# An attention and mixer kernel on one core: the planner's durations and hand-over times reset, and a new table of places

## The chip, the core and the metric

One core of a Trainium2 chip runs the whole program. Its engines work side by side, each through its own list of instructions in order: TensorE (PE in the profile: matrix products, and transposes as products with an identity), VectorE (DVE), ScalarE (ACT), GpSimd (POOL) and SyncE (SP, which issues most DMAs). An instruction waits until the semaphores of what it depends on are up; whatever is queued behind it on its engine waits too. The metric is device time in microseconds (us) of one execution.

## The reference

The input is a sequence of 2048 rows of 512 numbers. Two layers with the same weights follow one another, each of two parts:

- A: `x + attention(layernorm(x)) @ wo`. Queries, keys and values are `layernorm(x) @ wqkv`, 32 heads of 16. Row s attends to the 8 rows s, s-2, ..., s-14 (rows below 0 masked), by softmax.
- B: with y the sum that A returns, `x = y + B(layernorm(y))`. In B, `h = gelu(layernorm(y') @ w1)` of its input y'; the four quarters of h's columns are shifted by +1, -1, +2 and -2 rows and multiplied by w2; `x1 = y' + that`; the result is `x1 + gelu(layernorm(x1) @ w3) @ w4`, with 1792 hidden columns.

All in float32.

## The kernel before

The 2048 rows are four blocks of 512, each four tiles of 128 rows; with two layers that makes eight block passes, n = 0 to 7. A pass goes through these stages, which the names in the code follow:

- `p1_stream` (for n = 0: `p1_quarters`): normalise, turn the tiles by TensorE transposes (`turn_pe`, four 128x128 transposes, shown as `mm<-ident,f`), multiply by wqkv (`mm<-wq_hl,xt`), scale into `ev`, write to DRAM.
- `p2_unit`: attention on VectorE for a quarter of the heads at a time: a product of 128x2048 (`prod<-kv,q`), a reduction (`L<-prod`), softmax, a second product and additions; the result o is turned (`mm<-ident,o`) into oT.
- `p3`: wo product (`mm<-wo_hl,oT`), sum with x on VectorE, norm, transposes (into `nT`), w1 product (`mm<-nT,w_hl`), gelu, shifts on GpSimd.
- `p4`: w2 product (`mm<-w_hl,h`), sum, norm, transposes.
- `p5`: 14 chunks of w3 product (`mm<-nT,w`), gelu, and w4 product into four accumulators (`acc<-w,g`).

Numbers are split into a high and a low float16 part, and a product is three float16 products (`HLS`), so one 128x512 result takes 12 matmuls; such a dozen is called a group below. Where `p3` and `p4` normalise a tile, the chain is: a group on TensorE; the sum on VectorE (`scalar_tensor_tensor`, which also sums the row); the square on ScalarE (`sq_dev`, L646); three tiny GpSimd instructions for the inverse root and the shift (`power`, L652; in the profile `b` in `p3` and `c` in `p4`); the normalised rows on ScalarE (`normed`, L665, writing `f`, or `prod` where a buffer is lent); four transposes on TensorE; eviction into `nT` on ScalarE. Whatever TensorE has queued between the group and the transposes covers that chain.

At the start the weights are scaled by a power of two and split (`small_weight`, `big_pair`), beside the first block's attention.

What sets the order: the code builds about 3150 operations (`Graph.__call__`, L210). Operation number k gets as its key the k-th number of the table `PLACES`. `plan` (L253) then plays the program forward: five engines, each with a time at which it is free; an operation is ready when its predecessors have ended and a hand-over time has passed; a free engine starts the ready operation of the lowest key whose buffers are to be had. Each operation's duration is the number given where it is made. `LAT` is the hand-over time, `LAT_PE` that to TensorE and `LAT_SP` that to SyncE from another engine. GpSimd operations, and VectorE operations marked "lock", exclude one another in the plan (`port`). Some operations may run on either of two engines, and the plan's choice is kept. The instructions are emitted in the order in which the plan starts them, and class `InOrder` (L360) holds each engine to it. The plan's times reach the chip only as this order. All instructions carry one line in the profile, that of `issue` (L370 before, L372 in the changed kernel), so they are told apart by their tiles.

Of the kernel before, what the change touches and what calls it, by code (L numbers as in the profile page):

```python
# [12 lines left out]
AF = mybir.ActivationFunctionType  # L13
ALU = mybir.AluOpType
# [6 lines left out]
D = 512  # L21
F = 1792
NB = 4
NT = 4
NC = D // P
# [180 lines left out]
class Graph:  # L206
# [3 lines left out]
    def __call__(self, key, alts, r=(), w=(), after=(), xfer=0.0):  # L210
# [30 lines left out]
        for b in o.touch:  # L241
            b.users += 1
            b.left += 1
        self.ops.append(o)
        return o


LAT, LAT_PE, LAT_SP, LAT_DMA, TABLE = 0.12, 0.4, 0.3, 2.3, 1.3
FREE = (7.0, 1.0, 1.5, 1.0, 1.1)
LANES = 8  # L250


def plan(ops, slots):  # L253

# [1121 lines left out]
```

## Time and profile before

| | |
|---|---|
| three runs | 1204.16, 1207.10, 1209.59 us; median 1207.1 |
| profiled execution, span | 1203.0 us, 15906 instructions |
| busy PE / DVE / ACT / POOL | 1178.4 / 926.1 / 639.6 / 355.9 us |
| stages of the span | 0 to 34 start; 34 to 132 weights and first attention; 132 to 205 first `p3`, `p4`; 205 to 431 passes 0 to 1 and the start of 2; 431 to 1198 the rest; 1198 to 1203 last store |

A row of the timeline gives start, duration, engine, operation, output tile, input tiles, and in brackets how long the engine stood idle before it and what ended that. Neighbouring like instructions are merged (x24 is two groups). Ends of matmuls are modelled and a little late: the spacing of starts is what TensorE took.

### The profile page before, as it was taken

The numbers are of one execution on the slowest core, as the hardware profiler recorded it, in microseconds if no ns is written. First come the engines' busy times: TensorE is split into PE (matmuls) and PEld (weight loads), VectorE is DVE, ScalarE is ACT, GpSimd is POOL, SyncE is SP. The second block draws the span as 40 slices with busy tenths as digits, with TensorE's granted clock in tenths as the row PEclk, the third lists the DMA queues.
The fourth block names the chain that finished last, engine by engine and source line by source line (L and its number), as shares of the span: only waits on it lengthen the run. The fifth ranks groups of instructions, "written<-read, shape, count | busy, mean of one in ns | idle before, by whom it ended". The sixth has DMA issues, their size and how long they took to land.

```text
span 1203.0 us, 15906 instructions
## 1 busy us (share of the span) xinstructions
PE 1178.4 (98%) x5652; PEld 586.9 (49%) x5652; DVE 926.1 (77%) x1082; ACT 639.6 (53%) x1118; POOL 355.9 (30%) x512
## 2 busy tenths in 40 slices
PE   8998999999999999999999999999999999999998
PEld 6544444554444445444444444444444444445554
DVE  4899898999899989888883799889897989324212
ACT  5755675236864374565564556544654554544331
POOL 4231344005611355143531163113612350221000
PEclk9999999999999999999999999999999999999999
DMA  7677775576695554554355446656248534111322
GB/s 204 200 214 203 217 201 143 158 201 166 187 273 171 156 148 100 157 138 118 100 149 134 138 130 179 173 140 171 60 140 188 150 101 149 62 53 66 102 79 62
DMA packets 129839, 176.77 MB, mean 147 GB/s; under 512 B 11704, under 2 KB 73144, under 8 KB 129760
## 3 DMA queue, kind: packets, MB, share of 16 engines
q1 hardware_dynamic: 127504, 173.86, 51.8%
q10 hardware_dynamic: 2256, 1.90, 0.6%
q8 instruction: 44, 0.72, 0.2%
q14 instruction: 35, 0.29, 0.1%
HBM read 132.64 MB, written 37.87 MB: 142 GB/s over the span
## 4 chain that ended last, share of the span: by engine, by line
PE 90%; DMA 3%; ACT 3%; POOL 1%; DVE 1%; issue 1%; SPq 1%; ACTq 0%; POOLq 0%; DVEq 0%
PE mm L370 67%; PE acc L370 24%; DMA w<-in_A_x_dram 1%; ACT junk L370 1%; SPq L370 1%; DMA h<-in_A_wqkv_dram 1%; DMA x<-in_A_x_dram 0%; DMA nT<-in_A_wqkv_dram 0%; ACT ev L370 0%; ACT f L370 0%; POOL c L370 0%; POOL x L370 0%; DMA w<-in_B_w_dram 0%; POOL b L370 0%; ACT xt L370 0%
## 5 line engine op out<-in xcount | busy, mean ns | idle before, releaser
L370 PE MATMUL acc<-w,g 128*128 128x512 f16 (+1 forms) x1260 | 307.6, 393 | 0.1
L370 PE MATMUL mm<-nT,w 128*128 128x512 f16 (+1 forms) x1288 | 304.6, 390 | 0.9 <-ACT nT L370 0.9
L370 PE MATMUL mm<-wq_hl,xt 128*128 128x512 f16 x1008 | 226.7, 381 | 3.8 <-ACT ev L370 3.8
L370 ACT ACTIVATE mm<-mm,s_w 128x512 f32<-128x512 f32 (+1 forms) x144 | 90.6, 630 | 207.3 <-PE mm L370 206.6
L370 PEld LDWEIGHTS <-w 128*128 128x128 f16 x1344 | 125.0, 98 | 136.6
L370 PEld LDWEIGHTS <-g 128*128 128x128 f16 x1176 | 115.0, 98 | 129.3
L370 PEld LDWEIGHTS <-xt 128*128 128x128 f16 x1008 | 99.2, 99 | 118.6 <-issue 7.3
L370 DVE TENSOR_TENSOR prod<-kv,L 128x2048 f32<-128x2048 f32 x64 | 147.2, 2299 | 0.8
L370 DVE TENSOR_REDUCE L<-prod 128x128 f32<-128x2048 f32 x64 | 145.9, 2281 | 0.5
L370 DVE TENSOR_TENSOR prod<-kv,q 128x2048 f32<-128x2048 f32 x58 | 134.0, 2310 | 3.3 <-DMA kv<-kv_d 2.3
L370 DVE TENSOR_TENSOR prod<-prod 128x1024 f32<-128x1024 f32 (+1 forms) x129 | 134.4, 1042 | 2.7
L370 POOL TENSOR_TENSOR g<-f,g 128x512 f16<-128x512 f32 x32 | 46.4, 1452 | 172.6 <-ACT f L370 103.2
L370 PE MATMUL mm<-nT,w_hl 128*128 128x512 f16 x384 | 87.9, 379 | 1.8 <-ACT nT L370 1.4
L370 PE MATMUL mm<-w_hl,h 128*128 128x512 f16 x384 | 86.0, 379 | 0.0
L370 PE MATMUL mm<-wo_hl,oT 128*128 128x512 f16 x384 | 85.3, 379 | 0.0
L370 DVE SCALAR_TENSOR_TENSOR g<-mm,c_g,g 128x512 f16<-128x512 f32 x56 | 41.8, 747 | 55.8 <-ACT g L370 55.7
L370 POOL TENSOR_SCALAR b<-b 128x1 f32<-128x1 f32 (+1 forms) x48 | 20.4, 425 | 191.2 <-ACT junk L370 189.4
L370 DVE TENSOR_TENSOR nT<-mm,nT 128x512 f16<-128x512 f32 x60 | 40.8, 687 | 45.1 <-ACT nT L370 44.5
L370 ACT ACT_TABLE_LOAD x54 | 69.3, 1283 | 6.6 <-issue 3.6
L370 ACT ACTIVATE ev<-mm,s_kv 128x512 f32<-128x512 f32 x56 | 38.3, 684 | 62.1 <-PE mm L370 49.4
L370 ACT ACTIVATE g<-mm,c_g 128x512 f16<-128x512 f32 x98 | 66.9, 685 | 2.0
L370 POOL COPY h<-h 128x126 f16<-128x126 f16 (+3 forms) x56 | 42.8, 786 | 81.7 <-DVE h L370 79.7
(189 smaller groups left out, 1408.0 us busy)
## 6 DMA issues: line engine op xcount, KB each, us to landing
w<-w SPq DMA_DIRECT2D x196, 256.0 KB
kv<-kv_d SPq DMA_DIRECT2D x112, 352.0 KB
w<-in_B_w_dram SPq DMA_DIRECT2D x56, 256.0 KB
kv_d<-ev SPq DMA_DIRECT2D x112, 128.0 KB
q_d<-ev SPq DMA_DIRECT2D x28, 256.0 KB
q<-q_d SPq DMA_DIRECT2D x28, 256.0 KB
w<-g SPq DMA_DIRECT2D x28, 256.0 KB
x<-x SPq DMA_DIRECT2D x27, 256.0 KB
```

Source lines behind the costliest of these rows:

```text
L370: i = f(*a, **k).ins
```

## The change

Three things change. The planner's hand-over times get smaller, and a new tuple `TAIL` separates when an engine is free again from when its result is there: a TensorE result is there 0.165 us after the engine is free; VectorE and ScalarE are free 0.085 and 0.115 us before their operation's end. Many operations get another duration, mostly by a few per cent. The table `PLACES` is replaced as a whole. The operations themselves, their number, tiles and buffers stay; a few that may run on either of two engines change engine.

```
 PLACES = [int(k) for k in """
-132 128 130 133 14 4 88 15 106 8 113 5 114 108 120 157 16 9 0 2 1 12 13 23
+1048 846 385 293 3 10 80 104 83 867 97 788 368 333 442 412 321 438 732 946 114 620 605 108
...
-LAT, LAT_PE, LAT_SP, LAT_DMA, TABLE = 0.12, 0.4, 0.3, 2.3, 1.3
+LAT, LAT_PE, LAT_SP, LAT_DMA, TABLE = 0.06, 0.12, 0.1, 2.3, 1.3
+TAIL = (0.165, 0.085, 0.115, 0.0, 0.0)
...
-                free[e] = o.end = begin + d
+                o.end = begin + d + (TAIL[PE] if e == PE else 0.0)
+                free[e] = o.end - TAIL[e]
...
-        pe(key, 0.4, lambda: T.matmul(ps.t[:, :n], ones, ssv, start=True, stop=True), [ss], [ps])
+        pe(key, 0.14, lambda: T.matmul(ps.t[:, :n], ones, ssv, start=True, stop=True), [ss], [ps])
...
-        dve(key, 0.06 + n * 0.00137, lambda: V.scalar_tensor_tensor(
+        dve(key, 0.23 + n * 0.00101, lambda: V.scalar_tensor_tensor(
...
-        act(key, 0.73, lambda: A.activation(junk, src(), AF.Square, bias=tot.t[:, k:k + 1], scale=-float(D),
+        act(key, 0.815, lambda: A.activation(junk, src(), AF.Square, bias=tot.t[:, k:k + 1], scale=-float(D),
...
-        gp(key, 1.2, fn, [(ss, j), (tot, k)], [(ve, i), (r, i), (nb, i)])
+        gp(key, 1.24, fn, [(ss, j), (tot, k)], [(ve, i), (r, i), (nb, i)])
...
-        gp(key + 0.2, 2.3, r1_of, [(ss, tiles), (sums, tiles)], [(r1, tiles), ve1, (nb1, tiles)])
+        gp(key + 0.2, 1.93, r1_of, [(ss, tiles), (sums, tiles)], [(r1, tiles), ve1, (nb1, tiles)])
...
-                pe(key, 12 * wd * 0.00042 + 0.02, up,
+                pe(key, 12 * (wd * 0.000417 + 0.0025), up,
...
-                pe(key, 0.65 * (k1 - k0), down, [w4, (g, [0, 1])], acc[k0:k1])
+                pe(key, 0.6478 * (k1 - k0), down, [w4, (g, [0, 1])], acc[k0:k1])
```

The order, at three places. A row is an instruction: line, operation, output, inputs, shape. The second and later matmuls of a group and their weight loads are left out.

First, TensorE at the second norm of block 0 (`p4`, n = 0; at 186 to 203 us of the trace before): w_hl,h are the w2 groups of three tiles, ident,f the transposes of the normalised tiles, wq_hl,xt groups of the fourth block's p1_stream, and nT,w the first w3 product, which needs all three transposed tiles. Before:

```order
L370 MATMUL mm_69<-w_hl,h_260 128x512
...
L370 MATMUL mm_67<-ident,f_268 128x128 x4
...
L370 MATMUL mm_71<-wq_hl,xt_284 128x512
...
L370 MATMUL mm_67<-wq_hl,xt_288 128x512
...
L370 MATMUL mm_69<-ident,f_258 128x128 x4
L370 MATMUL mm_71<-ident,f_287 128x128 x4
L370 MATMUL mm_65<-nT_249,w_280 128x384 x4
```

The same place now:

```order
L372 MATMUL mm_65<-wq_hl,xt_287 128x512
...
L372 MATMUL mm_69<-w_hl,h_260 128x512
...
L372 MATMUL mm_67<-w_hl,h_260 128x512
...
L372 MATMUL mm_71<-w_hl,h_260 128x512
...
L372 MATMUL mm_65<-ident,f_286 128x128 x4
L372 MATMUL mm_69<-ident,o_295 128x128 x4
...
L372 MATMUL mm_67<-wq_hl,xt_284 128x512
...
L372 MATMUL mm_65<-ident,f_268 128x128 x4
L372 MATMUL mm_71<-ident,f_257 128x128 x4
L372 MATMUL mm_69<-nT_249,w_254 128x384 x4
```

One of the two wq groups has moved ahead of the three w2 groups, and the transposes of o, which stood among the w2 groups, have moved in behind the last of them.

Second, TensorE at the first norm of block 2 (`p3`, n = 2; at 417 to 431 us before): wo_hl,oT is the end of the last wo group, ident,f and ident,prod the normalised tiles, acc groups are w4 products of block 1, and nT,w_hl is the first w1 group. Before:

```order
L370 MATMUL mm_65<-wo_hl,oT_302 128x512
...
L370 MATMUL mm_71<-ident,f_265 128x128 x4
...
L370 MATMUL acc_306<-w_255,g_259 128x512
...
L370 MATMUL mm_67<-ident,f_258 128x128 x4
L370 MATMUL mm_69<-ident,o_295 128x128 x4
...
L370 MATMUL acc_306<-w_279,g_262 128x512
...
L370 MATMUL mm_65<-ident,prod_285 128x128 x4
L370 MATMUL mm_71<-ident,f_287 128x128 x4
...
L370 MATMUL mm_67<-nT_274,w_hl 128x512
```

Now:

```order
L372 MATMUL mm_67<-wo_hl,oT_300 128x512
L372 MATMUL mm_71<-ident,f_286 128x128 x4
L372 MATMUL mm_65<-ident,o_295 128x128 x4
...
L372 MATMUL acc_306<-w_274,g_269 128x512
...
L372 MATMUL mm_67<-ident,prod_285 128x128 x4
...
L372 MATMUL acc_306<-w_250,g_299 128x512
...
L372 MATMUL mm_71<-ident,f_265 128x128 x4
...
L372 MATMUL acc_306<-w_254,g_266 128x512
...
L372 MATMUL mm_65<-nT_270,w_hl 128x512
```

Between the last two sets of transposes now stands an acc group, and another one between the last set and the first w1 group; the first tile's transposes have moved in among the wo groups.

Third, the first norm of block 6 (`p3`, n = 6; at 911 to 927 us before). TensorE from the first wo group to the first tile's transposes, before:

```order
L370 MATMUL mm_71<-wo_hl,oT_296 128x512
...
L370 MATMUL mm_69<-wo_hl,oT_296 128x512
...
L370 MATMUL acc_305<-w_248,g_259 128x512
...
L370 MATMUL mm_67<-wo_hl,oT_296 128x512
...
L370 MATMUL mm_65<-nT_274,w_270 128x512
...
L370 MATMUL acc_305<-w_250,g_269 128x512
...
L370 MATMUL mm_71<-ident,f_261 128x128 x4
```

Now, with what follows:

```order
L372 MATMUL mm_67<-wo_hl,oT_298 128x512
...
L372 MATMUL mm_71<-wo_hl,oT_298 128x512
...
L372 MATMUL mm_65<-wo_hl,oT_298 128x512
...
L372 MATMUL mm_69<-ident,f_257 128x128 x4
...
L372 MATMUL acc_304<-w_278,g_258 128x512
```

VectorE there, up to the sums of the first two wo groups (x with s_wo), before and now:

```order
L370 TENSOR_TENSOR prod_281<-kv_286,q_263 128x2048
L370 SCALAR_TENSOR_TENSOR g_266<-mm_65,c_g,g_266 128x512
L370 TENSOR_REDUCE L_292<-prod_281 128x16x8
L370 SCALAR_TENSOR_TENSOR x_291,b_0_168<-mm_71,s_wo,x_291 128x512
L370 TENSOR_TENSOR prod_281<-kv_267,q_301 128x2048
L370 SCALAR_TENSOR_TENSOR x_290,b_0_168<-mm_69,s_wo,x_290 128x512
```

```order
L372 SCALAR_TENSOR_TENSOR g_269<-mm_65,c_g,g_269 128x512
L372 TENSOR_TENSOR prod_281<-kv_264,q_263 128x2048
L372 SCALAR_TENSOR_TENSOR x_291,b_0_168<-mm_67,s_wo,x_291 128x512
L372 TENSOR_REDUCE L_282<-prod_281 128x16x8
L372 SCALAR_TENSOR_TENSOR x_289,b_0_168<-mm_71,s_wo,x_289 128x512
```

Two groups instead of five stand behind the first wo group's end and ahead of its tile's transposes, and the sum follows the product directly.

## Rows read from the trace of the kernel before

**Rows 1.** The page's head: span, and busy time, share and instructions by engine.

```profile
span 1203.0 us, 15906 instructions
PE 1178.4 (98%) x5652; PEld 586.9 (49%) x5652; DVE 926.1 (77%) x1082; ACT 639.6 (53%) x1118; POOL 355.9 (30%) x512
```

**Rows 2.** Busy time by stretch: length, busy by engine, granted clock, DMA share, GB/s.

```profile
33.70:132.00 98.30, 91.47 (x409) 46.61 (x408) 90.70 (x96) 58.28 (x134) 23.77 (x35) 0.98 0.74 198
132.00:205.00 73.00, 68.79 (x335) 34.25 (x334) 66.59 (x92) 51.92 (x94) 37.47 (x53) 0.99 0.68 193
205.00:431.00 226.00, 221.38 (x931) 110.25 (x930) 200.66 (x233) 118.94 (x204) 60.27 (x80) 1.00 0.66 185
431.00:1198.00 767.00, 766.87 (x3830) 373.26 (x3828) 551.22 (x631) 390.72 (x640) 220.41 (x300) 1.00 0.43 122
114.50:118.00 3.50, 3.50 (x12) 1.48 (x11) 3.43 (x5) 1.21 (x3) 0.30 (x1) 0.51 0.83 211
203.30:206.80 3.50, 3.50 (x7) 1.92 (x6) 2.47 (x2) 0.00 (x0) 0.00 (x0) 0.51 1.04 239
```

**Rows 3.** TensorE's waits: for what, us in total, times, longest.

```profile
PE mm L370 <- ACT f L370: 5.7, 5, 2.0
```

**Rows 4.** VectorE's waits from 33.7 to 132 us.

```profile
DVE xt L370 <- ACT xt L370: 2.9, 2, 2.5
DVE prod L370 <- DMA kv<-x: 1.4, 1, 1.4
```

**Rows 5.** Timeline of TensorE at block 0's second norm.

```profile
193.96 0.60 PE L370 MATMUL mm<-ident,f 128*128 128x128 f32 x4
194.40 5.34 PE L370 MATMUL mm<-wq_hl,xt 128*128 128x512 f16 x24
199.58 0.60 PE L370 MATMUL mm<-ident,f 128*128 128x128 f32 x4
201.29 0.66 PE L370 MATMUL mm<-ident,f 128*128 128x128 f32 x4 [1.11 <-ACT f L370]
```

**Rows 6.** Timeline of GpSimd there.

```profile
189.46 1.27 POOL L370 TENSOR_TENSOR x<-x,f 128x512 f32<-128x512 f32 x1 [3.94 <-DVE f L370]
...
192.49 3.25 POOL L370 TENSOR_TENSOR x<-x,f 128x512 f32<-128x512 f32 x1 [0.46 <-DVE f L370]
...
196.75 0.27 POOL L370 TENSOR_SCALAR c<-c,c 128x1 f32<-128x1 f32 x1
...
198.02 2.37 POOL L370 TENSOR_SCALAR c<-c,c 128x1 f32<-128x1 f32 x1
```

**Rows 7.** Timeline of VectorE there.

```profile
189.29 2.28 DVE L370 TENSOR_REDUCE L<-prod 128x128 f32<-128x2048 f32 x1
...
192.32 2.29 DVE L370 TENSOR_TENSOR prod<-kv,q 128x2048 f32<-128x2048 f32 x1
...
198.05 2.28 DVE L370 TENSOR_TENSOR prod<-kv,q 128x2048 f32<-128x2048 f32 x1
```

**Rows 8.** Timeline of TensorE at block 2's first norm.

```profile
429.37 0.66 PE L370 MATMUL mm<-ident,f 128*128 128x128 f32 x4 [2.04 <-ACT f L370]
430.72 3.48 PE L370 MATMUL mm<-nT,w_hl 128*128 128x512 f16 x14 [0.69 <-ACT nT L370]
```

**Rows 9.** Timeline of TensorE at 333 us.

```profile
333.00 0.63 PE L370 MATMUL mm<-ident,f 128*128 128x128 f32 x4 [0.63 <-DVE xt L370]
```

**Rows 10.** Timeline of TensorE at block 6's first norm.

```profile
911.30 5.34 PE L370 MATMUL mm<-wo_hl,oT 128*128 128x512 f16 x24
...
926.84 0.60 PE L370 MATMUL mm<-ident,f 128*128 128x128 f32 x4
```

**Rows 11.** Timeline of VectorE there.

```profile
914.99 0.74 DVE L370 SCALAR_TENSOR_TENSOR g<-mm,c_g,g 128x512 f16<-128x512 f32 x1
...
917.84 0.74 DVE L370 SCALAR_TENSOR_TENSOR x<-mm,s_wo,x 128x512 f32<-128x512 f32 x1
```

**Rows 12.** Timeline of GpSimd there.

```profile
921.58 0.27 POOL L370 TENSOR_SCALAR b<-b,b 128x1 f32<-128x1 f32 x1
```

More of the change, by code (lines that the diff above doesn't have):

```diff
@@ L572, in bound @@
             V.tensor_scalar(f2.t[:, :m], v, 1e-30, 1e30, ALU.max, ALU.min)
-        dve(key, 0.2, bound, [ps], [f2])
+        dve(key, 0.16, bound, [ps], [f2])
         p = inv.t[:, :m] if inv.kind is None and not isinstance(inv.t, tuple) else inv.t
-        gp(key, 0.9, lambda: G.tensor_tensor(p, f2.t[:, :m], nhalf[:, :m], ALU.pow), [f2], [inv])
+        gp(key, 1.03, lambda: G.tensor_tensor(p, f2.t[:, :m], nhalf[:, :m], ALU.pow), [f2], [inv])
         def cut():
@@ L603, in hi_of @@
         h = hi if callable(hi) else lambda a: hi
-        op(key, [(ACT, 0.2 + n * 0.00103, lambda: A.activation(h(0), src(), AF.Copy, scale=scale), None),
-                 (POOL, 0.12 + n * 0.00125, lambda: G.tensor_scalar(
+        op(key, [(ACT, 0.186 + n * 0.00103, lambda: A.activation(h(0), src(), AF.Copy, scale=scale), None),
+                 (POOL, 0.14 + n * 0.00115, lambda: G.tensor_scalar(
                      h(0), src(), scale, 1.0, ALU.mult, ALU.mult), None)], r, w)
     def rest(key, lo, src, scale, hi, n, r, w):
-        dve(key, 0.06 + n * 0.00137, lambda: V.scalar_tensor_tensor(
+        dve(key, 0.23 + n * 0.00101, lambda: V.scalar_tensor_tensor(
             lo(), src(), scale, hi(), ALU.mult, ALU.subtract), r, w, lock=True)
@@ L668, in normed @@
         f = lambda e: (lambda: e.tensor_scalar(n.t, src(), r.t[:, s], nb.t[:, s], ALU.mult, ALU.add))
-        op(key, [(ACT, 0.82, lambda: A.activation(n.t, src(), AF.Identity, bias=nb.t[:, s],
+        op(key, [(ACT, 0.805, lambda: A.activation(n.t, src(), AF.Identity, bias=nb.t[:, s],
                                                   scale=r.t[:, s]), None),
@@ L682, in fn @@
                 T.transpose(ps.t[:, f], n.t[:, f], ident)
-        pe(key, 0.44, fn, rd, [ps, (dst, "new"), *new])
+        pe(key, 0.437, fn, rd, [ps, (dst, "new"), *new])
         split(key, ps, dst, cells, hi, lo, scale)
@@ L693, in fn @@
                 T.transpose(ps.t[:, f], n.t[:, f], ident)
-        pe(key, 0.44, fn, [n], [ps, (dst, "new")])
+        pe(key, 0.437, fn, [n], [ps, (dst, "new")])
         act(key, 0.6, lambda: A.activation(out(), ps.t.rearrange("p (c t) -> p c t", c=NC), AF.Copy), [ps], cell)
@@ L704, in split @@
         else:
-            act(key, 0.72, lambda: A.activation(hi(), pv(), AF.Copy, scale=scale.t), [ps, scale], [hc])
+            act(key, 0.69, lambda: A.activation(hi(), pv(), AF.Copy, scale=scale.t), [ps, scale], [hc])
             dve(key, 0.75, lambda: V.scalar_tensor_tensor(
@@ L724, in p1_norm @@
         if l == 0 and b >= STATS:
-            act(key, 0.64, lambda: A.activation(junk, src(), AF.Identity, accum_out=tot.t[:, i:i + 1]),
+            act(key, 0.725, lambda: A.activation(junk, src(), AF.Identity, accum_out=tot.t[:, i:i + 1]),
                 [x], [(tot, i)])
@@ L778, in fn @@
                                      start=(c == 0), stop=(c == NC - 1))
-                    pe(key, 0.86 * len(ks), fn, [xts[i], *[stage_of(int(qt > 0), c) for c in range(NC)]],
+                    pe(key, 0.864 * len(ks), fn, [xts[i], *[stage_of(int(qt > 0), c) for c in range(NC)]],
                        [ps, *[(d, "new") for d in dst]])
@@ L817, in fn @@
                             m += 1
-                pe(key + 0.01 * j, 2.6, fn, [(xt, both), (wq, wq_all)], [ps])
+                pe(key + 0.01 * j, 2.591, fn, [(xt, both), (wq, wq_all)], [ps])
                 act(key, 0.7, lambda ps=ps, ev=ev, sc=sc: A.activation(
@@ L902, in big_pair @@
                 dma(key - 0.5, v, lambda i=i: w4_d[P * i:P * (i + 1), :], [], [t], 0.8, begun)
-            act(key, 0.64, lambda v=v, m=m: A.activation(
+            act(key, 0.725, lambda v=v, m=m: A.activation(
                 junk, v(), AF.Square, accum_out=ss_p[c].t[:, m:m + 1]), [t], [(ss_p[c], m)])
@@ L1096, in fn @@
                         m += 1
-            pe(key + 0.01 * i, 2.6, fn, [*[(t, both) for t in oTs[n]], x, (wo, whole)], [ps],
+            pe(key + 0.01 * i, 2.591, fn, [*[(t, both) for t in oTs[n]], x, (wo, whole)], [ps],
                after=[w2_last[n - 1]] if n else [])
@@ L1132, in fn @@
                         m += 1
-            pe(key + 0.1, 2.6, fn, [(nT, [(i, a) for i in range(NT) for a in range(2)]), (w1, whole)],
+            pe(key + 0.1, 2.591, fn, [(nT, [(i, a) for i in range(NT) for a in range(2)]), (w1, whole)],
                [ps, (h, "new")])
@@ L1214, in fn @@
                         j += 1
-            w2_last[n] = pe(key + 0.01 * k, 2.6, fn, [(h, h_cells(i)), (w2, whole)], [ps])
+            w2_last[n] = pe(key + 0.01 * k, 2.591, fn, [(h, h_cells(i)), (w2, whole)], [ps])
             dve(key, 0.75, lambda ps=ps, x1=x1, s=s: V.scalar_tensor_tensor(
@@ L1251, in down @@
                          start=(c == 0), stop=(c == NF - 1))
-        pe(key, NC * K * 0.214, up, [w3, (nT, [(k, 0) for k in range(K)])], [ps, (g, "new")])
+        pe(key, NC * K * 0.215, up, [w3, (nT, [(k, 0) for k in range(K)])], [ps, (g, "new")])
         act(key, 0.15 + 0.115 * K, lambda: A.activation(f32v(g.t, D)[:, :P * K], ps.t[:, :P * K],
                                                        AF.Gelu_apprx_tanh, scale=1.0 / SN), [ps], [g], cls=GELU)
-        pe(key, 0.857 * K, down, [w4, g], acc)
+        pe(key, 0.8585 * K, down, [w4, g], acc)
     def p5(n):
```

262 rows, old and new, of the table PLACES are left out of this document.

## The prediction

> **What bounds the kernel now.** I read the page's engine line first. TensorE is busy 1178.4 us of a span of 1203.0, 98% [rows 1]; VectorE, the next, 926.1. So TensorE's own work is the floor, and since the change adds and drops no matmul, all that an order can move is the 24.6 us in which TensorE stands still (1203.0 - 1178.4), and whatever new standing still it makes.
>
> Second, busy time by stage [rows 2], to see where that stillness lies. From 33.7 to 132 us (preparing the weights, first attention block) TensorE misses 6.8 us (98.30 - 91.47), from 132 to 205 us 4.2 (73.00 - 68.79), from 205 to 431 us 4.6 (226.00 - 221.38), and from 431 to 1198 us 0.13 (767.00 - 766.87). The remaining 8.8 us are the loads at the start and the last store. The reader should see two kernels in one: 431 us with 15.6 us of holes, then 767 us with none to win. In the first stage VectorE is busy 90.70 of 98.30 us, nearly as much as TensorE.
>
> Third, the waits. TensorE's largest kinds include ACT f, the normalised rows that its transposes read: 5.7 us in five places, the longest 2.0 [rows 3]. VectorE's two largest waits between 33.7 and 132 us are 2.9 for xt and 1.4 for a DMA [rows 4], 4.3 us in all. Two holes are followed by a lower clock: granted 0.51, the 1.2 GHz level, for 3.5 us at 114.5 and for 3.5 us at 203.3 [rows 2]. At half speed each costs about 1.7 us beyond the hole itself (an estimate: 3.5 x 0.49).
>
> **The change part by part.** Durations, TAIL and LAT exist only inside the planner; what reaches the chip is the order of instructions. I therefore price the places where the order differs, against the profiled execution of 1203.0 us. Its median sits 4.1 us higher, at 1207.1 (1207.1 - 1203.0); I add that at the end.
>
> *Start and tail.* TensorE's first operations stand as before and the last stores hang on the last w4 product as before: 0.
>
> *33.7 to 132 us.* In the new order four short VectorE operations precede the first xt subtraction and fill part of its 2.5 us wait. But the second xt subtraction now precedes the product that used to wait 1.4 us for a DMA [rows 4]; it waits for its own ScalarE copy, so the wait moves on. I take 0. Bounds: -4.3 if both go, +2.5 if the longest is met once more. The value 0 is nearest to the row of the DMA wait, whose source no reordering of VectorE brings forward.
>
> *The second layer norm of block 0, at 194 to 203 us.* Before, between the third w2 group's end and the third set of f transposes stand one set of transposes, two 2.59 us groups and a second set. The two groups run from 194.40 to 199.58 [rows 5], 2.59 each; a set takes 0.44 (193.96 to 194.40). Cover: 0.44 + 5.18 + 0.44 = 6.06. That is not enough, and TensorE stands 1.11 before the third set. In the new order one of the two groups has gone ahead of the w2 groups, where TensorE did not wait in any case, and a set of o transposes stands in its place: 0.44 + 0.44 + 2.59 + 0.44 = 3.91. Cover shrinks by 2.15, so the wait grows from 1.1 to 3.3: **+2.2**. What might take this back is GpSimd. Its last step for the third tile took 2.37 us at 198.02, against 0.27 for the same step at 196.75 [rows 6], and beside it VectorE ran a product of two SBUF operands from 198.05 [rows 7]. If they miss each other, 2.1 us go (2.37 - 0.27). Bounds: +0.1 (2.2 - 2.1), down to -1.1 if the wait goes with it, and +4.3 if one more step is caught. I take +2.2, because VectorE's operations here keep their sequence and start from the same groups.
>
> The Trainium skill bears on this in "SBUF — State Buffer", section "Who interferes with whom": VectorE and GpSimd share a pair of ports under an exclusive lock; a VectorE instruction with two SBUF inputs contends with a GpSimd instruction that reads SBUF, the one that comes first holding it for its whole length, while tensor_reduce does not contend. The trace agrees: 2.37 against 0.27 us beside a product, and an addition of 3.25 us at 192.49 against 1.27 at 189.46, where VectorE was in a reduction [rows 6, 7]. The rule speaks against the change, whose planner books this three-instruction step as one piece of 1.24 us that a product cannot cut into. By the rule the stretch costs +2.2, without it +0.1.
>
> *205 to 431 us.* At the fourth tile of block 2, TensorE stands 2.04 before its transposes and 0.69 before the first w1 group [rows 8]. New: a 2.59 us w4 group stands between the two, which covers the 0.69 (**-0.7**); ahead of the transposes the cover falls from 6.93 to 6.50, one set of four less (**+0.4**). At 333.0 a wait of 0.63 for an xt half [rows 9] goes, since two 2.59 us groups now stand there (**-0.6**). The others stay. Sum -0.9; bounds -4.6 (every hole of the stage) and +2.1 (one more step caught).
>
> *431 to 1198 us.* Nothing can be won: 0.13 us is idle. But the cover is thinner in places. The first tile of block 6 is the clearest. Its wo product is the first of two groups that begin at 911.30, so it ends near 913.9; its VectorE sum starts at 917.84, GpSimd is done at 921.85 (921.58 + 0.27), and the transposes, at 926.84, wait for nothing [rows 10 to 12]. From GpSimd's end to transposes it needed 0.90 at the other place (201.29 less 198.02 + 2.37) [rows 5, 6], so the chain needed 921.85 + 0.90 - 913.9 = 8.9. Before, 12.95 covered it (five groups); now two groups, 5.18. On VectorE the new order puts the sum directly behind the product, without the subtraction and the reduction that stood between; the sum could then start where that subtraction started, at 914.99 [rows 11], 2.85 earlier: need 6.0, wait **+0.8**. Three more places get thin: 7.77 to 5.18, 7.77 to 4.37, 10.80 to 5.18 us of cover. By the same need, less whatever queue goes, they may cost nothing. Bounds: 0, and +8.4 (four places, a 2.1 us collision in each). I take +0.8.
>
> Sum: 0 + 2.2 - 0.9 + 0.8 = +2.1 on 1203.0, so 1205.1; with 4.1 for the median, **1209**.
>
> **Rivals.**
> *The early holes close (faster).* A planner with shorter hand-overs packs the first 431 us better than my few places show. For it: 15.6 us of holes and 2 x 1.7 us of lowered clock, 19.0 in all, lie there, and VectorE's 4.3 us of waits in its fullest stage can be a matter of order. Against it: VectorE is 92% busy there (90.70 / 98.30), the DMA it waits for is not brought forward, and one of TensorE's waits grows. It is measurably faster once a third is won (1203.0 + 4.1 - 6.3 = 1200.8). At two thirds, 12.7: 1203.0 - 12.7 + 4.1 = 1194.
>
> *Thin hand-overs (slower).* With less cover, every GpSimd step caught by a VectorE product (2.1 us) ends in a wait of TensorE, and after 431 us there was none before. For it: the 2.37 and 3.25 us rows, and cover cut at four places I counted. Against: at most of the others cover stays above the 8.9 us that the slow chain needed. From two catches beyond my sum it is measurably slower (1209.2 + 4.2 = 1213.4); five give 1209.2 + 10.5 = 1219.7, about 1220.
>
> *Nothing of it shows.* Holes merely change places, because TensorE's 1178.4 us are fixed and the first stage ends when VectorE's work does: 1207. This is the forecast's neighbour and has its answer, no change.
>
> **How the numbers follow.** A measurement of this kernel can tell about 0.5%, 6 us: faster is below 1201.1, slower above 1213.1. Forecast, with holes moved or slightly larger (1201 to 1213): 0.43. Early holes close: 0.30. Thin hand-overs: 0.24. The remaining 0.03 I split between the ends: faster 0.31, same 0.43, slower 0.26. The range from 1193 to 1220 takes in two thirds of the first rival and five catches of the second; the likeliest case by itself spans 1202 to 1213.
>
> **What would show each step.** In the changed profile I look at: idle time in the four stages (I expect about 6.8, 6.4, 3.7 and 0.9 us, from the holes above and the terms); a wait of about 3.3 us for ACT f before the third set of f transposes of block 0's second norm, and beside it a GpSimd step of 2 us or more; no wait between the fourth tile's transposes and the first w1 group of block 2; and a wait of under 1 us at block 6's first tile. If the first two stages together lose less than 7 us, the first rival holds. If more than 3 us are idle between 431 and 1198 us, the second does. The forecast is wrong if block 0's wait does not grow, or if VectorE leaves the first stage several us earlier.

## The result, and the profile after

The changed kernel takes 1210.95 us (median of 7 runs, 1209.2 to 1214.3), the kernel before, run beside it, 1204.49 (7 runs). The ratio is 1.0045, 95% interval 1.0029 to 1.0061: by it the change costs 5.4 us, which is clear of the noise and yet just inside the 0.5% that was called no change. The profiled span went from 1203.0 to 1208.0 us.

The page's head, as in [rows 1]:

```profile
span 1208.0 us, 15875 instructions
PE 1180.2 (98%) x5652; PEld 587.3 (49%) x5652; DVE 928.5 (77%) x1083; ACT 635.3 (53%) x1115; POOL 355.2 (29%) x508
```

Busy time by stretch, as in [rows 2]; the last three rows are the stretches with a lowered clock:

```profile
33.70:132.00 98.30, 92.57 (x415) 47.92 (x413) 92.54 (x97) 58.26 (x136) 27.86 (x35) 0.98 0.75 198
132.00:205.00 73.00, 67.09 (x327) 33.16 (x328) 64.30 (x90) 52.71 (x95) 36.31 (x51) 0.98 0.67 193
205.00:431.00 226.00, 222.52 (x929) 110.62 (x929) 207.90 (x237) 119.63 (x205) 60.95 (x80) 0.99 0.67 185
431.00:1198.00 767.00, 763.48 (x3812) 370.76 (x3811) 544.43 (x625) 383.37 (x632) 216.47 (x298) 1.00 0.44 121
...
10.70:14.10 3.40, 3.17 (x8) 2.59 (x9) 1.68 (x4) 1.74 (x3) 1.91 (x7) 0.52 0.95 300
92.90:96.30 3.40, 3.32 (x11) 1.80 (x12) 3.30 (x7) 1.43 (x3) 0.00 (x0) 0.56 0.82 207
202.80:209.60 6.80, 6.08 (x14) 3.51 (x15) 4.45 (x4) 1.22 (x3) 0.36 (x1) 0.58 0.54 145
```

TensorE's holes of over 0.6 us from 90 us on, from its timeline:

```profile
92.98 1.12 PE L372 MATMUL mm<-ident,f 128*128 128x128 f32 x4 [2.66 <-DVE xt L372]
...
114.87 5.32 PE L372 MATMUL mm<-wq_hl,xt 128*128 128x512 f16 x23 [1.72 <-DVE xt L372]
132.03 0.66 PE L372 MATMUL mm<-ident,o 128*128 128x128 f32 x4 [0.71 <-ACT ev L372]
153.78 0.66 PE L372 MATMUL mm<-ident,f 128*128 128x128 f32 x4 [1.85 <-ACT f L372]
199.46 0.66 PE L372 MATMUL mm<-ident,f 128*128 128x128 f32 x4 [0.60 <-ACT f L372]
202.83 1.12 PE L372 MATMUL mm<-ident,f 128*128 128x128 f32 x4 [2.72 <-ACT f L372]
204.64 5.73 PE L372 MATMUL mm<-nT,w 128*128 128x384 f32 x11 [0.69 <-ACT nT L372]
293.98 0.59 PE L372 MATMUL mm<-nT,w_hl 128*128 128x512 f16 x2 [0.95 <-ACT nT L372]
334.83 0.39 PE L372 MATMUL mm<-ss_p,ones 128*128 128x4 f32 x2 [1.00 <-ACT junk L372]
...
984.54 0.66 PE L372 MATMUL mm<-ident,f 128*128 128x128 f32 x4 [1.63 <-ACT f L372]
1016.27 2.76 PE L372 MATMUL mm<-nT,w 128*128 128x512 f16 x12 [1.28 <-DMA w<-w]
```

A hole is a time in which TensorE stands idle. Counted by operation (every hole over 0.3 us behind 34 us in the two timelines, so that a hole at a stage's edge stays with its stage), this is where the 5.0 us of the span come from:

| TensorE loses | before | after | forecast | measured |
|---|---|---|---|---|
| holes, first attention (up to its last transposes) | 6.8 | 4.9 | 0 | -1.9 |
| holes, from there to block 0's w3 | 4.2 | 6.6 | +2.2 | +2.4 |
| holes, to block 2's w1 | 4.1 | 2.9 | -0.9 | -1.2 |
| holes, the rest | 0 | 3.3 | +0.8 | +3.3 |
| lowered clock, 1.7 us per 3.4 us (an estimate: half speed) | 2 times | 4 times, one of them at 10.7 us | 0 | +3.4 |

The sum is 5.8 us (2.4 of holes, added before rounding, and 3.4); TensorE's last instruction ends 5.2 us later, since part of the lowered clock fell on moments when TensorE stood still (6.08 of 6.80 us busy in the last row above). Of the clock's 3.4 only 1.7, net, stand behind holes of the new order: the stretch at 10.7 us does not come from the order (last section). One execution is a poor measure of the clock (see b_gp40 below). The mean over runs is a better one: it is 0.9941 over the changed kernel's 7 runs and 0.9962 over 23 later runs of the kernel before; the difference, 0.0021 of 1208 us, is 2.5 us, about half of the loss (an estimate, which counts stretches near the start too). The clock also explains most of the spread between runs of one kernel: those of the kernel before at 0.995 average 1206.9 us, at 0.997 1204.1.

GpSimd and VectorE at the place of the first term, block 0's second norm, to be compared with [rows 6, 7]:

```profile
194.03 3.25 POOL L372 TENSOR_TENSOR x<-x,f 128x512 f32<-128x512 f32 x1 [0.32 <-DVE f L372]
...
198.29 0.27 POOL L372 TENSOR_SCALAR c<-c,c 128x1 f32<-128x1 f32 x1
...
199.56 2.37 POOL L372 TENSOR_SCALAR c<-c,c 128x1 f32<-128x1 f32 x1
```

```profile
190.32 0.75 DVE L372 SCALAR_TENSOR_TENSOR prod<-mm,s_w,prod 128x512 f32<-128x512 f32 x1 [0.30 <-PE mm L372]
...
193.86 2.29 DVE L372 TENSOR_TENSOR prod<-kv,q 128x2048 f32<-128x2048 f32 x1
...
199.59 2.29 DVE L372 TENSOR_TENSOR prod<-kv,q 128x2048 f32<-128x2048 f32 x1
```

Both collisions are there again, with the same lengths: 3.25 and 2.37 us, each beside a product.

### The profile page after: what moved, and what is told of

It reads as the page before. It is cut to its first block, busy times and chain, and to the rows that moved or that the text cites. A ratio compares the mean times of both kernels' runs of the same rounds, so it can differ in the third digit from the quotient of the medians.

```text
span 1208.0 us, 15875 instructions
## 1 busy us (share of the span) xinstructions
PE 1180.2 (98%) x5652; PEld 587.3 (49%) x5652; DVE 928.5 (77%) x1083; ACT 635.3 (53%) x1115; POOL 355.2 (29%) x508
## 4 chain that ended last, share of the span: by engine, by line
PE 80%; DVE 9%; DMA 5%; ACT 2%; POOL 1%; issue 1%; SPq 1%; ACTq 0%; DVEq 0%; POOLq 0%
PE mm L372 59%; PE acc L372 21%; DVE prod L372 4%; DVE L L372 2%; DMA kv<-kv_d 1%; DMA w<-w 1%; ACT junk L372 1%; SPq L372 1%; DVE nT L372 1%; POOL c L372 1%; DMA h<-in_B_w_dram 1%; DMA nT<-in_A_wqkv_dram 1%; ACT f L372 0%; POOL x L372 0%; DVE h L372 0%
## 5 line engine op out<-in xcount | busy, mean ns | idle before, releaser
L372 POOL TENSOR_TENSOR g<-f,g 128x512 f16<-128x512 f32 x35 | 54.7, 1563 | 194.0 <-ACT f L372 93.2
L372 POOL TENSOR_SCALAR b<-b 128x1 f32<-128x1 f32 (+1 forms) x48 | 16.2, 338 | 181.8 <-ACT junk L372 179.9
L372 PEld LDWEIGHTS <-oT 128*128 128x128 f16 x426 | 41.6, 98 | 50.2 <-issue 2.3
```

What stands on the lines that cost most here:

```text
L372: i = f(*a, **k).ins
```

## Experiments

To move single operations and nothing else, `plan` was made to start on each engine only the head of a given list. Given either kernel's own lists it keeps that kernel's order.

```
-            if free[e] > now or not ready[e]:
+            if free[e] > now or head[e] == len(TURN[e]) or TURN[e][head[e]] not in ready:
                 continue
...
+            got = ops[TURN[e][head[e]]]
```

Every ratio is against runs of the kernel before on the same chip, with its 95% interval; the changed kernel itself stands at 1.0045.

| run | median, us | ratio |
|---|---|---|
| ba500 | 1211.94 | 1.0052 (1.0036 to 1.0068) |
| ab500 | 1225.4 | 1.0162 (1.0144 to 1.0181) |
| a_gp40 | 1207.36 | 1.0017 (1.0006 to 1.0028) |
| b_gp40 | 1203.79 | 0.9984 (0.9973 to 0.9996) |
| a_cover | 1209.3 | 1.0031 (1.0021 to 1.0041) |
| a_gp46_sp56 | 1207.87 | 1.0025 (1.0014 to 1.0036) |
| a_all | 1202.84 | 0.9985 (0.9973 to 0.9996) |
| a_all_act30 | 1204.15 | 0.9988 (0.9974 to 1.0002) |
| b_gp40_act32 | 1199.8 | 0.9953 (0.9937 to 0.9969) |

A difference between two rows has the noise of both. Against the changed kernel, a_gp40 is faster by 0.0028 with about 0.0019 to either side, a_gp46_sp56 by 0.0020 with 0.0019, a_cover by 0.0014 with 0.0019, which is not clear of zero.

### The two halves: ba500 and ab500

Lists joined: one kernel's operations up to 500 us of its plan, then the other's order (in short; the kernels hold the numbers).

```
+TURN[e] = [o for o in first[e] if start(o) < 500] + [o for o in second[e] if not yet in the list]
```

> Order of the kernel before for all that its plan starts before 500 us (up to the second norm of block 2), the changed kernel's order for the rest; each engine takes its list strictly. Theory (two halves): the changed kernel loses in both halves, here only what it loses late: the wait of 1.6 us before the second tile's transposes in block 6's second norm and the 1.3 us wait for a w3 load near 1016 us. So 2.9 us above the kernel before, about 1207.4; TensorE idle under 0.3 us more up to 430 us, two windows of lowered clock, near 115 and 203 us. Rival (early only): the late waits are paid back elsewhere, time within 1 us of the kernel before. Rival (late only): 5 us above it.

> The other way round: the changed kernel's order for what its plan starts before 500 us, then the order of the kernel before. Two halves: 2 to 3 us above the kernel before (holes -1.8, +2.4, -1.2 in the three early stages, and two more windows of lowered clock, 1.7 us each, the first partly beside waiting for VectorE), about 1207; four windows of lowered clock; no wait over 1 us after 500 us. Early only: 5 us above. Late only: within 1 us of the kernel before.

Both totals miss the 1207 us that was expected and can't be used: the seam itself costs. In ab500 TensorE waits 10.3 us at 528 us for a weight load and 2.6 at 535 for another, two thirds of its 20 us; in ba500 three small waits stand at the seam. The stretch away from the seam can. TensorE's late holes in ba500, and TensorE from 600 to 1198 us in ab500:

```profile
987.18 0.66 PE L365 MATMUL mm<-ident,f 128*128 128x128 f32 x4 [1.64 <-ACT f L365]
1018.94 1.25 PE L365 MATMUL mm<-nT,w 128*128 128x512 f16 x5 [1.31 <-DMA w<-w]
```

```profile
600.00:1198.00 598.00, 598.00 (x2991) 291.46 (x2989) 412.74 (x476) 304.20 (x497) 162.44 (x227) 1.00 0.43 122
```

With the new order late, both holes are there although everything early is old; with the old order late there is none although everything early is new. So the late 2.9 us belong to the new order of the second half and not to something carried over.

### GpSimd's addition: a_gp40 and b_gp40

GpSimd's list at block 0's second norm, the same edit in the changed kernel and in the one before:

```
 addition to x, tile 1
 three-instruction step, tile 1
-addition to x, tile 2
 three-instruction step, tile 2
 three-instruction step, tile 3
+addition to x, tile 2
 addition to x, tile 3
```

> The changed kernel, with one GpSimd instruction moved: in block 0's second norm the addition to x of the second tile goes behind the three-instruction steps of the second and the third tile. Nothing else moves. Theory (collision): the 3.25 us addition and the 2.37 us last step no longer stand in the chain; the wait of 2.7 us before the third set of transposes falls to under 0.7, and the lowered clock after it goes from 7 us to 3.4 or none: 2.5 to 5 us faster than the changed kernel, 1206 to 1208.5. Rival (cover): with one group less ahead of the transposes VectorE's sums are late anyway; the wait falls by less than 0.8 and the time by less than 1 us. Rival (moved): the step meets another VectorE product and the wait stays.

> The same single move in the kernel before. Collision: its 1.11 us wait before the third transposes goes, and the 0.89 behind it stays or grows; if the clock then does not fall at 203 us, 1.7 us more: 1 to 3 us faster than the kernel before. Cover or moved: no change (within 0.5 us).

Both agree with the collision. GpSimd in a_gp40, and TensorE there:

```profile
199.41 0.27 POOL L365 TENSOR_SCALAR c<-c,c 128x1 f32<-128x1 f32 x1
199.64 4.54 POOL L365 TENSOR_TENSOR x<-x,f 128x512 f32<-128x512 f32 x2
```

```profile
200.99 0.66 PE L365 MATMUL mm<-ident,f 128*128 128x128 f32 x4 [1.04 <-ACT f L365]
202.34 1.15 PE L365 MATMUL mm<-nT,w 128*128 128x384 f32 x2 [0.69 <-ACT nT L365]
```

The last step takes 0.27 instead of 2.37 us, the waits of 0.60 and 2.72 become 1.04 in all, and 3.4 us of lowered clock follow instead of 6.8. The ratio falls by 0.0028, 3.4 us, and the mean clock over its runs is 0.9963 against 0.9941. In b_gp40 the wait of 1.11 [rows 5] is gone and the clock is granted in full from 203 to 207 us, where before it was 0.51; 1.9 us faster by its ratio. Two stretches of b_gp40, as in [rows 2]:

```profile
203.30:206.80 3.50, 3.50 (x12) 1.97 (x11) 3.11 (x4) 2.83 (x4) 0.00 (x0) 1.00 0.98 251
427.60:431.00 3.40, 3.40 (x9) 1.16 (x8) 3.40 (x9) 1.67 (x5) 1.03 (x3) 0.50 0.98 272
```

The second stretch warns against reading the clock from one execution. It stands behind the same 2.04 us wait as in the kernel before [rows 8], where the clock did not fall; and the fall at 114.5 us, behind a wait of 1.50 us before, is missing in b_gp40 behind one of 1.51. Over its 12 runs b_gp40's mean clock is 0.9962, as in the kernel before, so no gain by the clock is shown for it.

### Cover: a_cover

```
 TensorE's list
-wq group
 w2 groups of three tiles
 transposes of f, tile 1; of o; wq group
+wq group
 transposes of f, tiles 2 and 3
```

The group's eviction on ScalarE and its two DMAs on SyncE move with it.

> The changed kernel, with the wq group that it moved ahead of block 0's w2 groups put back behind them, ahead of the second set of transposes (with its ScalarE eviction and its two DMAs). Theory (cover): the wait before the third set, 2.7 us, falls by most of a group's 2.59, to under 0.7, though GpSimd's 2.4 us step is still there; the lowered clock behind it shortens from 7 to 3.4 us or goes: 2 to 4 us faster than the changed kernel. Rival (the w2 groups now wait): the group had covered a wait for the shifts of h, and the hole appears ahead of the w2 groups: under 1 us faster. Rival (GpSimd alone): the wait stays above 2 us.

This one went against my theory. TensorE and VectorE there:

```profile
195.18 0.66 PE L365 MATMUL mm<-ident,f 128*128 128x128 f32 x4 [1.42 <-ACT f L365]
...
203.39 0.66 PE L365 MATMUL mm<-ident,f 128*128 128x128 f32 x4 [1.50 <-ACT f L365]
204.94 1.24 PE L365 MATMUL mm<-nT,w 128*128 128x384 f32 x3 [0.89 <-ACT nT L365]
```

```profile
188.68 2.29 DVE L365 TENSOR_TENSOR prod<-kv,q 128x2048 f32<-128x2048 f32 x1
190.89 0.74 DVE L365 SCALAR_TENSOR_TENSOR prod<-mm,s_w,prod 128x512 f32<-128x512 f32 x1
```

The third wait falls from 2.72 to 1.50, but a new one of 1.42 stands before the first transposes: 3.8 us in all, against 4.0 in the changed kernel. The w2 groups began earlier (185.8 against 187.5), but VectorE does not: its product still runs when the first one is done, and the first sum starts at 190.89. From that sum to the third transposes it is 12.50 us here and 12.51 in the changed kernel (190.32 to 202.83), but 10.0 in a_gp40 (190.98 to 200.99). The chain hangs on VectorE and GpSimd; where a TensorE group stands only decides before which transposes TensorE waits. Of the 1.7 us that the ratio falls (1.0045 to 1.0031, within the noise), the holes explain little; the mean granted clock rose to 0.9965. Why it did is not settled: in its profiled execution the clock did not fall behind the 1.50 us wait, in a_gp40's it fell behind the 1.04.

### The late waits: a_gp46_sp56

The two waits have two causes in the changed kernel's trace. GpSimd's last step of block 6's second tile, and VectorE beside it:

```profile
978.08 1.65 POOL L372 TENSOR_TENSOR x<-x,f 128x512 f32<-128x512 f32 x1 [3.53 <-DVE f L372]
...
980.74 2.90 POOL L372 TENSOR_SCALAR c<-c,c 128x1 f32<-128x1 f32 x1
```

```profile
980.71 0.68 DVE L372 TENSOR_TENSOR x<-x,f 128x512 f32<-128x512 f32 x1
981.31 2.28 DVE L372 TENSOR_TENSOR prod<-kv,q 128x2048 f32<-128x2048 f32 x1
```

And SyncE's queue, where the load that TensorE misses (it landed 4.0 us after its issue at 1012.20) stands behind three stores of the output:

```profile
1010.36 1.74 SPq L372 DMA_DIRECT2D out_dram<-x  x3
1012.20 0.53 SPq L372 DMA_DIRECT2D w<-w  x1
```

```
 GpSimd               SyncE
-addition, tile 2     -three stores of block 5's output
 step, tile 2          load of w3
+addition, tile 2     +three stores of block 5's output
```

> The changed kernel with two single moves late in the program: on GpSimd, in block 6's second norm, the addition to x of the second tile goes behind that tile's three-instruction step; on SyncE, the load of one w3 tile goes ahead of three stores of block 5's output. Theory: both late waits (1.6 us at 984, 1.3 us at 1016) go and the time falls by 2.9 us to about 1208, the early stages as in the changed kernel. Rival for the first: the step meets a VectorE product again and the wait stays. Rival for the second: the load waits for its buffer, not for the stores, and lands no earlier.

Both holes are gone: there is none above 0.3 us behind 444 us, and the step's last instruction takes 0.26, beside a reduction:

```profile
982.93 0.26 POOL L365 TENSOR_SCALAR c<-c,c 128x1 f32<-128x1 f32 x1
```

The ratio falls by 0.0020, 2.4 us.

### All of it, and one queue more: a_all, a_all_act30

> The changed kernel with all four moves: the GpSimd addition behind the steps in block 0's and in block 6's second norm, the wq group back, the w3 load ahead of three stores. If the holes add up: 3.6 us (measured for the first move), up to 1 us more for the group, 2.9 us for the late two: about 1203.5, within 0.3% of the kernel before. If what is left of the slowdown sits elsewhere, it stays above 1206.

The gains nearly add up, as far as their noise lets one say: 0.0060, 7.2 us, against 7.5 (3.4 + 1.7 + 2.4) by the single ratios, and the mean clock is 0.9978. The changed kernel is then a little faster than the one before, by 0.0015 (0.0004 to 0.0027).

```
 ScalarE's list at block 0's first norm
+normalise tile 2
 eviction ev; copy xt; square of a w3 tile; square of tile 4
-normalise tile 2
```

> The changed kernel with the four moves and a fifth: on ScalarE, in block 0's first norm, the normalising of the second tile goes ahead of an eviction, an xt copy and two squares that stood before it though its GpSimd step had ended 2.5 us earlier. Theory (a queue, not a collision): the 1.85 us wait before that tile's transposes at 154 us falls under 0.5, VectorE, which waits 2.6 us for the same transposes, runs on, and the end of the program comes 1 to 2 us sooner: 1201 to 1202. Rival (VectorE): the next sums are behind VectorE's products in any case, the hole moves to the second norm, and under 0.5 us is won.

The 1.85 us hole at 154 us went, but two smaller ones came just behind it:

```profile
156.50 0.36 PE L365 MATMUL mm<-ss_p,ones 128*128 128x4 f32 x2 [0.57 <-DVE nT L365]
157.62 0.66 PE L365 MATMUL mm<-ident,f 128*128 128x128 f32 x4 [0.77 <-ACT ev L365]
```

No gain shows: the ratio is 0.9988 against 0.9985, though the noise of the two, 0.0018, could hide one of 1 to 2 us. The trace speaks for the rival, in another form: the hole did not move to the second norm, where the two waits are 1.42 and 0.88 us as in a_all, but VectorE gets there no sooner. VectorE's last addition of block 0's attention, and its first sum of the second norm, in a_all_act30:

```profile
130.90 0.43 DVE L365 TENSOR_TENSOR o<-prod 128x256 f32<-128x256 f32 x1
...
189.95 0.74 DVE L365 SCALAR_TENSOR_TENSOR prod<-mm,s_w,prod 128x512 f32<-128x512 f32 x1
```

From the end of the one to the start of the other it is 58.6 us (189.95 - 131.33). In a_all, without the fifth move, it is 58.7 (188.39 less 129.24 + 0.42). The changed kernel takes 59.3 (190.32 less 130.64 + 0.42), the kernel before 56.8 (188.62 less 131.42 + 0.42). Closing this hole of TensorE brought VectorE forward by 0.1 us.

### The best version: b_gp40_act32

In the kernel before, the 2.04 us wait at 429 us [rows 8] is a collision as well: GpSimd's step for the fourth tile began at 425.29 with an instruction of 2.19 us, under the product that VectorE had begun at 425.15. It began that late because ScalarE's square stood behind an eviction that waited for TensorE. GpSimd and VectorE in the kernel before:

```profile
425.29 2.19 POOL L370 TENSOR_SCALAR b<-b 128x1 f32<-128x1 f32 x1 [2.89 <-ACT junk L370]
```

```profile
425.15 2.28 DVE L370 TENSOR_TENSOR prod<-kv,q 128x2048 f32<-128x2048 f32 x1
```

```
 ScalarE's list at block 2's first norm
+square of tile 4
 eviction of tile 2 into nT
-square of tile 4
```

> The kernel before with the GpSimd move in block 0's second norm and one more: on ScalarE, in block 2's first norm, the square of the fourth tile goes ahead of the eviction of the second tile's transposes, which waits for TensorE. Theory (collision): the fourth tile's GpSimd step then ends before VectorE's 2.3 us product starts, its 2.2 us instruction takes 0.2, and the 2.0 us wait before the fourth transposes goes: 2 us faster than with the first move alone, about 1201.8, and faster than both kernels. Rival: the transposes then wait for something else and under 0.7 us is won.

GpSimd and TensorE in it:

```profile
420.73 0.19 POOL L363 TENSOR_SCALAR b<-b 128x1 f32<-128x1 f32 x1 [0.89 <-ACT junk L363]
```

```profile
424.18 1.04 PE L363 MATMUL mm<-ident,prod 128*128 128x128 f32 x8
425.95 0.59 PE L363 MATMUL mm<-nT,w_hl 128*128 128x512 f16 x2 [0.74 <-ACT nT L363]
```

The third and fourth transposes stand in one row without a wait. The median is 1199.8 us, by the ratio 5.7 us faster than the kernel before: two operations, moved by two places and by one, win about as much as the whole new table loses. The second move won 3.7 us where 2 were expected; the mean clock rose to 0.9982, from 0.9962 in b_gp40.

## Why the prediction was right, and where it was not

The time, 1209, and the class, no change, came out right; the measured 1211 lies in the range. Term by term:

- **Block 0's second norm, +2.2.** Measured +2.0: the waits before and behind the last transposes grow from 1.11 + 0.89 [rows 5] to 0.60 + 2.72 + 0.69. That both collisions would come back was right. The size was luck, since the step's reason was half wrong: a_cover shows that the cover itself is worth 0.2 us, since the chain starts when VectorE gets to the first sum. VectorE gets there 2.5 us later, counted from its last addition (59.3 against 56.8); why it does stays open.
- **The clock, 0.** The step that failed most. I priced the two stretches before and carried them over, and let the longer wait leave the clock as it was. The 2.72 us wait was followed by 6.8 us at the 1.2 GHz level instead of 3.4, and a 2.66 us wait at 93 us by another 3.4, while the fall at 114.5 us did not come: +1.7 in this execution, about 2.5 by the mean clock of the runs. A given wait is not followed by a fall in every execution (b_gp40), so this term has to be priced from the mean of runs, not counted in one trace.
- **First attention, 0.** VectorE ends 0.8 us sooner (131.06 against 131.84) and TensorE's holes shrink by 1.9, inside the bounds of -4.3 and +2.5. So 0 was off by these 1.9. But the stage after it gave that back.
- **205 to 431 us, -0.9.** Measured -1.2, in other pieces. At block 2 both waits went, the 2.04 too, which I had let grow: GpSimd's step for the fourth tile now ran beside a reduction, and its first instruction took 0.19 us (at 424.88) instead of 2.19; the 0.63 at 333 us did not go but turned into 1.00 and 0.31.
- **After 431 us, +0.8.** Measured +3.3. The wait I named, at block 6's first norm, did not come: GpSimd was done at 919.16, 3.4 us behind the first wo group's end (913.22 + 2.59), where I had reckoned 5.1. One came in its second norm, by the mechanism of the second rival (an instruction of 2.90 us). The other late wait was in SyncE's queue, which I had not gone through.
- **The median, +4.1.** Mis-sized: in later runs the time lies 1.8 us above the span. This error and the missing clock mostly cancelled; with 1.8 I would have forecast 1207. That 1209 lies so near 1211 is luck in that measure.

The first rival, holes that close, was right for two stages and wrong for the total. The second was right in kind: one catch after 431 us, not five. By the signs I had set, idle times of 6.8, 6.4, 3.7 and 0.9 us by stage were expected and 5.7, 5.9, 3.5 and 3.5 came; the last is above the 3 us that were to speak for the second rival, though only 1.6 of it is a catch and 1.3 a late load.

The Trainium skill's rule ("SBUF — State Buffer", "Who interferes with whom") stood the tests: in all four places where a step was moved away from a product of two SBUF operands (a_gp40, b_gp40, a_gp46_sp56, b_gp40_act32), the instruction that had been caught went back to 0.2 to 0.3 us. In a_gp40 and b_gp40 another was caught for it, the first of the second tile's step, but only by a product's end: 0.84 and 0.99 us. The rule's other half shows too: in a_gp40 GpSimd's addition begins first, at 199.64, and VectorE's product takes 2.80 us instead of 2.29:

```profile
200.25 2.80 DVE L365 TENSOR_TENSOR prod<-kv,q 128x2048 f32<-128x2048 f32 x1
```

The recorded starts do not always tell who came first: in the changed kernel GpSimd's instruction is on record at 199.56, 0.03 us ahead of the product at 199.59, and yet it is the one that took longer.

## What to carry to other kernels

Before you trust a schedule planned from average durations, look in the trace for short instructions that took ten times their length, and ask what ran beside them; here, moving one addition on a side engine won 1.9 us, where 3150 new keys lost 5.4. When a wait seems to be short of cover, follow its chain back to the engine that starts it: moving TensorE's group changed the waits by 0.2 us while VectorE's queue set the start. And price the lowered clock that follows a longer wait, from the mean of many runs: here it was about half of the loss.

## What was not expected of the hardware

The clock fell near the program's start (0.52 from 10.7 us) in the changed kernel's profiled execution and, from 11 us, in those of a_gp40, b_gp40 and a_all_act30, and in none of the other seven, though TensorE's first 162 matmuls stand alike in all. It is not a matter of the order, and what decides it stays open.

It does delay what follows. TensorE's first row behind a wait after 34 us, in the kernel before, without the early fall, and in b_gp40, with it:

```profile
42.52 0.66 PE L370 MATMUL mm<-ident,f 128*128 128x128 f32 x4 [0.74 <-POOL f L370]
```

```profile
43.56 0.66 PE L363 MATMUL mm<-ident,f 128*128 128x128 f32 x4 [0.75 <-POOL f L363]
```

The order is the same up to there, and b_gp40 is 1.0 us behind; so it stays up to 114 us. That it still ended the first attention 0.6 us sooner (TensorE's transposes of o at 132.72 against 133.36) comes from the fall at 114.5 us, which the kernel before had and b_gp40 had not. Of the executions with the changed kernel's order, the three with the early fall reach their 163rd matmul at 37.5 us, the four without at 35.7 to 36.0 us.
